# Token blocks of 2, 2, 3, 3, 3, 3 tiles instead of eight of 2 in a fused S4 + SwiGLU layer

## The chip, the core and the metric

One core of a Trainium2 chip runs the whole program. The metric is the device time of one execution, in microseconds (us). The engines are TensorE (PE, matmuls; PEld is its weight load), VectorE (DVE), ScalarE (ACT), GpSimd (POOL) and SyncE (SP), which here issues every DMA. Each engine works through its own instructions in the order in which they were written; PE runs weight loads ahead of its matmuls.

## The reference

A layer with two residual branches over 2048 tokens of width 448; the scales and shifts (sa, ca, ga, sb, cb, gb) come from one conditioning row.

```python
mod = (_silu(c) @ w_mod).reshape(c.shape[0], 6, 1, -1)
h = _layernorm(x) * (1 + ca) + sa
x = x + ga * S4(h, ...)                       # y = causal conv of h with K, plus h * Dskip
h = _layernorm(x) * (1 + cb) + sb
x = x + gb * ((_silu(h @ w_gate) * (h @ w_up)) @ w_down)      # F = 1792
```

K[d, l] is the real part of a sum over 256 complex exponentials. For inputs whose exponents are small enough (a flag computed on the chip) the kernel uses the first two moments of K, so that the convolution becomes running sums over the tokens. That path, small_path, is the one that runs here.

## The kernel before

Tokens come in 16 tiles of 128. A prelude computes the modulation rows, the moments and the branch of tiles 0 and 1 and starts the weight loads. Then run_blocks takes the tiles in blocks of two (BLOCKS, L23). For each block, ffn runs over 14 slices f of 128 hidden columns. gate_up(f) makes the gate and the up product, transposed, in PSUM banks of their own: for each of the two, 11 matmuls whose moving operand is 128 x (128 per tile) values of hhi or hlo, the high and low parts of the normalised tokens (L659). Then come SiLU on ACT (L665, output p), the product on VectorE (L670), its high part on ACT (L673, phi) and its low part on VectorE (L674, plo). down(f-1) follows gate_up(f) on PE and adds phi and plo times the high and low parts of w_down to one bank dn per tile (L685, three matmuls of 448 columns for each tile). So the chain L665 to L674 of one f has the time of the next gate_up.

In block 0 (fresh) the weights of f+2 are also split into parts (split_w, L97 to L102, and split_d, L90 and L91), and pools.load sends the loads of f+5 and, for w_down, of f+3 through SyncE's queue, into three rotating stages each. The parts stay in SBUF for all later blocks. After block 0 the stages raw (4 KB a partition each) and rawd are no longer used.

The branch of the next block's tiles is woven in by hand. TIMES (L29) has one row for the first block and one for all others. A number h in it means f = h // 2, before down(f-1) if h is even and behind it if odd. The steps of one tile in small_path are:
- n1.stat and n1.root: mean and variance on VectorE (L128, L129), the root on GpSimd.
- s0: h, two operations on VectorE. s1: v0 and v1, the products with two gain rows (L774; on GpSimd, in block 0 on VectorE).
- s2: the running sums are added to row 0 of v0 (L779, VectorE) and of v1 (L780, GpSimd). Then v0 is split into vh (ACT) and vl (VectorE).
- s3: h times gd (L789, GpSimd, in block 0 VectorE).
- s4: three matmuls with the triangular matrix into the PSUM tile cv and a bank (L795 to L797), and an addition on VectorE.
- s14 takes the place of s2 to s4 in block 0 (L803 to L813): v0 and v1 unsplit, and two matmuls more that add the running sums on PE (L809, L810). A float32 matmul counts as two in the profile.
- s5: the new running sums (ACT L819, VectorE L820), sent to row 0 by a small DMA through SyncE's queue (L821), and two VectorE operations that finish the tile (L822, L823).
- n2.stat, n2.root and make_xn (ACT, L179): the second norm.

At f = 13, between gate_up(13) and down(12), transposes brings the next block's tiles into hhi and hlo: four groups, each into a PSUM tile, read by ACT (L187, L189) and VectorE (L191, L192). All four PSUM tiles come from bank(), four banks in rotation, which gate_up and s4 use too; each gate_up takes two. The other four banks are dn0, dn1, dn2 and cv. dn2 serves the first gate product and two small matmuls. In the prelude, cv is the output of the six L436 matmuls that come right behind the first transposes and make the first running sums.

At the end of a block VectorE scales and adds (L711, L712) and SyncE sends the tile out (L713). xbuf holds four token tiles; load_x (L63) loads the next block's tiles at the block's start.

Of the kernel before, what the change touches and what calls it, by code (L numbers as in the profile page):

```python
# [19 lines left out]
NF = F // 128  # L20
NP0 = 3
NS = 3
BLOCKS = [2] * 8  # L23
TILES = [list(range(sum(BLOCKS[:b]), sum(BLOCKS[:b + 1]))) for b in range(len(BLOCKS))]
MB = max(BLOCKS)

TIMES = (  # L29
    (3, (4, 6, 9, 10, 12), (7, 8, 16, 17, 18), 19, (20, 21)),  # L30
    (3, (4, 5, 9, 11, 12, 13, 14), (6, 8, 16, 17, 18, 19, 20), 21, (22, 23)),
)
EPS = 1e-5

# [4 lines left out]
def f32(ap):  # L39
    return ap.bitcast(F32)  # L40
# [3 lines left out]
def tile_kernel(ctx, tc, x, a_re, a_im, b_re, b_im, c_re, c_im, log_dt, dskip,  # L44
# [10 lines left out]
    def bank():  # L55
        t = psg.tile([128, 512], F32, name="bank")
        return t

    xs = {}
    xbuf = [const.tile([128, D], F32, name=f"x{q}") for q in range(2 * MB)]  # L60
    gb = const.tile([128, D], F32)

    def load_x(i):  # L63
# [6 lines left out]
    wgu, raw, wdn, wp = {}, {}, {}, {}  # L70
    stage = [const.tile([128, 2, 4, 128], F32, name=f"raw{q}") for q in range(NS)]
    stage_d = [const.tile([128, D], F32, name=f"rawd{q}") for q in range(NS)]

    def load_w(pool, j):
        wgu[j] = pool.tile([128, 2, 7, 128], F32R, name=f"gu{j}")
# [92 lines left out]

    xn = {}

    def make_xn(i, new, src=None, on_v=False):
        src = xs[i] if src is None else src
        xn[i] = new()
        m, rs, ng = n2.of[i]
        for o, a, n in ((0, 0, D), (D, 384, 64)):
            if on_v:
                ve.tensor_scalar(xn[i][:, o:o + n], src[:, a:a + n], m, rs, op0=OP.subtract, op1=OP.mult)
            else:
                sc.activation(xn[i][:, o:o + n], src[:, a:a + n], AF.Identity, scale=rs, bias=ng)  # L179

    def transposes(ts):
        n = len(ts) * 128
        for k in range(4):
            ps = bank()
            for j, i in enumerate(ts):
                pe.transpose(ps[:, j * 128:(j + 1) * 128], xn[i][:, k * 128:(k + 1) * 128], ident)  # L186
            sc.activation(hhi[:, k, 0:n], ps[:, 0:n], AF.Identity, scale=cb1c[:, k:k + 1], bias=sbc[:, k:k + 1])  # L187
            if k % 2:
                sc.activation(ps[:, 0:n], ps[:, 0:n], AF.Identity, scale=cb1c[:, k:k + 1], bias=sbc[:, k:k + 1])  # L189
            else:  # L190
                ve.tensor_scalar(ps[:, 0:n], ps[:, 0:n], cb1c[:, k:k + 1], sbc[:, k:k + 1], op0=OP.mult, op1=OP.add)  # L191
            ve.tensor_tensor(hlo[:, k, 0:n], ps[:, 0:n], f32(hhi[:, k, 0:n]), op=OP.subtract)  # L192
# [61 lines left out]
    with tc.tile_pool(name="pre", bufs=1) as pre, tc.tile_pool(name="wm", bufs=6) as wm:  # L254
# [164 lines left out]
        n2.root(TILES[0])  # L419
        mod_col(sbc, sb_, 0.0)  # L420
        for q in range(2):
            make_xn(q, lambda: pre.tile([128, 512], F32, name="xn", bufs=2), os[q], q == 0)
            if q == 0:
                sc.copy(xs[q], os[q])
                mod_col(cb1c, row, 1.0)
# [22 lines left out]
    def general_conv():  # L448
# [3 lines left out]
        with tc.tile_pool(name="gh", bufs=2) as gh:  # L452
            t = gh.tile([P, 4, D], F32, name="wga")
            sy.dma_start(t, w_group(2))
            sc.copy(g0, mod_row([t[:, k, :] for k in range(4)]))
            for i in range(NT):
                load_x(i)
                n1.all([i])
                h = gh.tile([128, D], F32, name="h")
                make_h(h, i)  # L460
                sy.dma_start(hd[i * 128:(i + 1) * 128, :], h)
# [172 lines left out]

    def run_blocks(pools, stages, first=None):
        work, hid = pools.work, pools.hid
        new_xn = lambda: work.tile([128, 512], F32, name="xn", bufs=MB)
        def ffn(ts, fresh, last, todo):
            n = len(ts) * 128
            dn = [psd.tile([128, 512], F32, name=f"dn{q}") for q in range(len(ts))]  # L640
# [3 lines left out]
            def gate_up(f, nw):  # L644
                head = fresh and f == 0
                if fresh and not head:
                    split_d(f)
                w = wgu[f]
                p = hid.tile([128, MB * 128], F32, name="p")
                hi = hid.tile([128, MB * 128], F32R, name="phi")  # L650
                lo = hid.tile([128, MB * 128], F32R, name="plo")
                ps = [psd.tile([128, 512], F32, name="dn2") if head else bank(), bank()]

                def mm(s, lo):

                    parts = ((0,), (1,), (2,), (6,)) if lo else ((0, 3), (1, 4), (2, 5), (6,))
                    for k, ws in enumerate(parts):
                        for a in ws:
                            pe.matmul(ps[s][:, 0:n], w[:, s, a], (hlo if lo else hhi)[:, k, 0:n],  # L659
                                      start=not lo and a == 0, stop=lo and k == 3)  # L660

                for s, z in ((0, False), (1, False), (0, True), (1, True)) if head else (
                        (0, False), (0, True), (1, False), (1, True)):
                    mm(s, z)
                sc.activation(p[:, 0:n], ps[0][:, 0:n], AF.Silu)  # L665
                if head:
                    split_d(f)
                elif nw is not None:
                    split_w(nw, 0)
                ve.tensor_tensor(ps[1][:, 0:n], p[:, 0:n], ps[1][:, 0:n], op=OP.mult)  # L670
                if nw is not None and not head:
                    split_w(nw, 1)
                sc.copy(hi[:, 0:n], ps[1][:, 0:n])  # L673
                ve.tensor_tensor(lo[:, 0:n], ps[1][:, 0:n], f32(hi[:, 0:n]), op=OP.subtract)  # L674
                if nw is not None:
                    split_w(nw, None if head else 2)
                pp[f] = hi, lo
# [25 lines left out]
            else:  # L703
                down(NF - 1, qz)
            for q, i in enumerate(ts):
                t = new_xn()[:, 0:D]

                h = D // 2 if last and q == len(ts) - 1 else D
                for a in range(0, D, h):
                    c_ = slice(a, a + h)  # L710
                    ve.tensor_tensor(t[:, c_], dn[q][:, c_], gb[:, c_], op=OP.mult)  # L711
                    ve.tensor_tensor(xs[i][:, c_], xs[i][:, c_], t[:, c_], op=OP.add)  # L712
                    sy.dma_start(out[i * 128:(i + 1) * 128, c_], xs[i][:, c_])  # L713
# [3 lines left out]
        if first is not None:  # L717
            for i in TILES[1]:
                load_x(i)
            for i in TILES[0]:  # L720
                first(i)
                n2.stat(i, TILES[0])
            n2.root(TILES[0])
            for i in TILES[0]:
                make_xn(i, new_xn)
            transposes(TILES[0])
        for b, ts in enumerate(TILES):
            todo = {}
            if b + 1 < len(TILES):
                nx = TILES[b + 1]  # L730

                def at(f, late, g, *a):
                    todo.setdefault((f, late), []).append((g, a))

                if b:
                    for i in nx:
                        at(0, 1, load_x, i)
                root1, *times, root2, shift = TIMES[min(b, 1)]
                st = stages(b == 0)

                def go(h, g, *a):
                    at(h // 2, h % 2, g, *a)

                for q, (i, hs) in enumerate(zip(nx, times)):
                    at(1 if b else q, 1, n1.stat, i, nx)
                    for h, g in zip(hs, st):
                        go(h, g, i)
                    go(hs[-1], n2.stat, i, nx)
                go(root1, n1.root, nx)
                go(root2, n2.root, nx)  # L750
                for h, i in zip(shift, nx):
                    go(h, make_xn, i, new_xn)
                at(NF - 1, 0, transposes, nx)
                if b == 0:
                    at(2, 1, end_gate)
            ffn(ts, b == 0, b + 1 == len(TILES), todo)

    def small_path(pools):
# [15 lines left out]
                (ve if on_v else po).tensor_tensor(v, h, g, op=OP.mult)  # L774
            vs[i] = h, v0, v1

        def s2(i):
            h, v0, v1 = vs[i]
            ve.tensor_tensor(v0[0:1], v0[0:1], run0[0:1], op=OP.add)  # L779
            po.tensor_tensor(v1[0:1], f32(v1[0:1]), run1[0:1], op=OP.add)  # L780
            vh = work.tile([128, D], F32R, name="vh")
            vl = work.tile([128, D], F32R, name="vl")
            sc.copy(vh, v0)
# [15 lines left out]
            vs[i] = o, s  # L799

        def s14(i):  # L803
            h, v0, v1 = vs[i]
            o = psd.tile([128, 512], F32, name="cv")[:, 0:D]
            s = bank()[:, 0:D]
            pe.matmul(o, f32(tri), v0, start=True, stop=False)
            pe.matmul(s, tri, v1, start=True, stop=False)
            pe.matmul(s, f32(tri[0:1, :]), run1[0:1], start=False, stop=True)  # L809
            pe.matmul(o, f32(tri[0:1, :]), run0[0:1], start=False, stop=True)  # L810
            s3(i, True)
            ve.tensor_tensor(xs[i], h, xs[i], op=OP.add)
            vs[i] = o, s  # L813
# [8 lines left out]
            ve.tensor_tensor(xs[i], xs[i], o, op=OP.add)  # L822
            ve.scalar_tensor_tensor(xs[i], s, tok, xs[i], op0=OP.mult, op1=OP.add)  # L823

        return lambda fresh: (s0, lambda i: s1(i, True), s14, s5) if fresh else (s0, s1, s2, s3, s4, s5)

    def general_path(pools, y):
        work = pools.work
# [17 lines left out]
            s0(i)  # L846
            s1(i)

        return lambda fresh: (s0, s1), first

    class Pools:
        def __init__(self, es):
# [56 lines left out]
```

## Time and profile before

| | |
|---|---|
| runs of the kernel (us) | 518.09, 519.38, 519.93; median 519.38 |
| the profiled execution | 519.4, its span 517.6 |
| prelude up to f=0 | 0 to 49.8 |
| block 0 | 49.8 to 113.9 |
| blocks 1 to 6 | 57.1 each |
| block 7, PE's part, and the rest | 456.5 to 510.2, and to 517.6 |
| mean granted PE clock | 0.982 |

The profile lists, for one execution, each engine's busy time, groups of instructions by source line with their shapes, waits with what ended them, and the chain of work that ended last, followed back from the end. In the chain, rows are start, length, and what ran; matmuls of one line in a row are merged, so that length divided by count is the spacing. A timeline row is start, length, engine, line, operation, output<-inputs, count and, in brackets, idle time before it with its releaser. A wait row is who waited <- for whom: total us, times, longest. A group row ends with busy us, mean ns of one, and idle us before it. Matmuls overlap, so the mean duration of one is longer than the spacing.

### The profile page before, as it was taken

The numbers are of one execution on the slowest core, as the hardware profiler recorded it, in microseconds if no ns is written. First come the engines' busy times: TensorE is split into PE (matmuls) and PEld (weight loads), VectorE is DVE, ScalarE is ACT, GpSimd is POOL, SyncE is SP. The second block draws the span as 40 slices with busy tenths as digits, with TensorE's granted clock in tenths as the row PEclk, the third lists the DMA queues.
The fourth block names the chain that finished last, engine by engine and source line by source line (L and its number), as shares of the span: only waits on it lengthen the run. The fifth ranks groups of instructions, "written<-read, shape, count | busy, mean of one in ns | idle before, by whom it ended". The sixth has DMA issues, their size and how long they took to land.

```text
span 517.6 us, 8533 instructions
## 1 busy us (share of the span) xinstructions
PE 493.8 (95%) x3371; PEld 461.8 (89%) x3371; DVE 286.1 (55%) x568; ACT 174.3 (34%) x414; POOL 102.0 (20%) x127
## 2 busy tenths in 40 slices
PE   7869999999999999999999999999999999999994
PEld 5446987999999999999998999989998999999993
DVE  2797797785553665455653655465555555252123
ACT  4347555552223322331225223331225222332110
POOL 1577000102311051103300051105210231100000
PEclk9977999999999999999999999999999999999998
DMA  7995455501000200010000200020000200010001
GB/s 209 277 220 160 138 157 153 166 15 58 2 2 0 73 1 0 2 48 26 0 2 1 71 1 2 2 71 2 2 2 0 72 1 0 3 37 1 0 2 42
DMA packets 26009, 26.15 MB, mean 51 GB/s; under 512 B 2248, under 2 KB 25288, under 8 KB 25960
## 3 DMA queue, kind: packets, MB, share of 16 engines
q1 hardware_dynamic: 25960, 25.52, 17.3%
q8 instruction: 28, 0.46, 0.4%
q14 instruction: 21, 0.17, 0.1%
HBM read 21.80 MB, written 3.67 MB: 49 GB/s over the span
## 4 chain that ended last, share of the span: by engine, by line
PE 90%; DVE 4%; DMA 2%; ACT 2%; issue 1%; SPq 0%; DVEq 0%
PE bank L659 56%; PE dn L685 26%; PE bank L203 2%; DMA dsk<-in_A_Dskip_dram 1%; PE dn L406 1%; PE bank L186 1%; DVE scr L350 1%; PE bank L236 1%; DMA run<-run 1%; DVE bank L670 1%; DVE plo L674 1%; DVE h L164 1%; ACT phi L673 1%; PE bank L796 0%; PE cv L797 0%
## 5 line engine op out<-in xcount | busy, mean ns | idle before, releaser
L659 PE MATMUL bank<-hhi,gu 128*128 128x256 f32 x1561 | 223.9, 283 | 0.0
L659 PEld LDWEIGHTS bank<-hhi,gu 128*128 128x128 f32 x1561 | 210.1, 191 | 4.2 <-ACT phi L673 0.7
L659 PE MATMUL bank<-hlo,gu 128*128 128x256 f32 x892 | 143.4, 283 | 0.0
L670 DVE TENSOR_TENSOR bank<-p,bank 128x256 f32<-128x256 f32 x112 | 47.9, 428 | 142.8 <-PE bank L659 141.7
L659 PEld LDWEIGHTS bank<-hlo,gu 128*128 128x128 f32 x892 | 123.1, 192 | 0.0
L673 ACT CAST phi<-bank 128x256 fp32r<-128x256 f32 x112 | 41.7, 372 | 144.8 <-DVE bank L670 144.8
L665 ACT ACTIVATE p<-bank 128x256 f32<-128x256 f32 x111 | 42.4, 382 | 129.2 <-PE bank L659 128.9
L674 DVE TENSOR_TENSOR plo<-bank,phi 128x256 fp32r<-128x256 f32 x112 | 47.4, 423 | 44.3 <-ACT phi L673 44.3
L685 PE MATMUL dn<-wdh,phi 128*128 128x448 f32 x224 | 64.9, 370 | 0.0
L685 PE MATMUL dn<-wdl,phi 128*128 128x448 f32 x224 | 63.9, 366 | 0.0
L685 PE MATMUL dn<-wdh,plo 128*128 128x448 f32 x224 | 63.8, 365 | 0.0
L685 PEld LDWEIGHTS dn<-wdh,plo 128*128 128x128 f32 x224 | 42.0, 188 | 3.5
L685 PEld LDWEIGHTS dn<-wdl,phi 128*128 128x128 f32 x224 | 42.0, 188 | 3.3
L685 PEld LDWEIGHTS dn<-wdh,phi 128*128 128x128 f32 x224 | 36.1, 191 | 1.7 <-ACT gu L98 0.7
L145 POOL TENSOR_SCALAR rsa<-mva 128x2 f32<-128x2 f32 x8 | 2.0, 251 | 143.3 <-DVE mva L129 143.3
L780 POOL TENSOR_TENSOR v<-v,run 1x448 fp32r<-1x448 f32 x12 | 13.8, 1146 | 49.6 <-DMA run<-run 49.6
L145 POOL TENSOR_SCALAR rsb<-mvb 128x2 f32<-128x2 f32 x8 | 1.8, 220 | 108.1 <-DVE mvb L129 108.1
L774 POOL TENSOR_TENSOR v<-h,gm 128x448 f32<-128x448 f32 x12 | 13.8, 1153 | 25.3 <-DVE h L166 25.3
L186 PE MATMUL bank<-ident,xn 128*128 128x128 f32 x64 | 10.9, 296 | 6.2 <-DVE plo L674 5.5
L203 PE MATMUL bank<-wmt,cs 112*128 112x448 f32 (+1 forms) x32 | 15.1, 624 | 1.6 <-DMA wmt<-in_w_mod_dram 1.6
L187 ACT ACTIVATE hhi<-bank,sbc,cb1c 128x256 fp32r<-128x256 f32 x32 | 16.5, 575 | 0.3 <-PE bank L186 0.3
L789 POOL TENSOR_TENSOR h<-h,gd 128x448 f32<-128x448 f32 x12 | 16.4, 1365 | 0.0
(178 smaller groups left out, 437.3 us busy)
## 6 DMA issues: line engine op xcount, KB each, us to landing
wmt<-in_w_mod_dram SPq DMA_DIRECT2D x6, 784.0 KB
x<-in_A_u_dram SPq DMA_DIRECT2D x16, 224.0 KB
out_dram<-x SPq DMA_DIRECT2D x15, 224.0 KB
rawd<-in_B_w_down_dram SPq DMA_DIRECT2D x14, 224.0 KB
raw<-in_B_w_gate_dram SPq DMA_DIRECT2D x14, 192.0 KB
raw<-in_B_w_up_dram SPq DMA_DIRECT2D x14, 192.0 KB
raw<-in_B_w_gate_dram SPq DMA_DIRECT2D x14, 64.0 KB
raw<-in_B_w_up_dram SPq DMA_DIRECT2D x14, 64.0 KB
```

The lines of the kernel that those rows point to most:

```text
L186: pe.transpose(ps[:, j * 128:(j + 1) * 128], xn[i][:, k * 128:(k + 1) * 128], ident)
L187: sc.activation(hhi[:, k, 0:n], ps[:, 0:n], AF.Identity, scale=cb1c[:, k:k + 1], bias=sbc[:, k:k + 1])
L203: pe.matmul(ps[0:rows, 0:D], cs[:, k:k + 1].to_broadcast([P, rows]), w[k], start=k == 0, stop=k == 3)
L659: pe.matmul(ps[s][:, 0:n], w[:, s, a], (hlo if lo else hhi)[:, k, 0:n], start=not lo and a == 0, stop=lo and k == 3)
L665: sc.activation(p[:, 0:n], ps[0][:, 0:n], AF.Silu)
L670: ve.tensor_tensor(ps[1][:, 0:n], p[:, 0:n], ps[1][:, 0:n], op=OP.mult)
L673: sc.copy(hi[:, 0:n], ps[1][:, 0:n])
L674: ve.tensor_tensor(lo[:, 0:n], ps[1][:, 0:n], f32(hi[:, 0:n]), op=OP.subtract)
L685: pe.matmul(dn[q][:, 0:D], u[:, cs], v, start=f == 0 and z == 0, stop=f == NF - 1 and z == 2)
L774: (ve if on_v else po).tensor_tensor(v, h, g, op=OP.mult)
L780: po.tensor_tensor(v1[0:1], f32(v1[0:1]), run1[0:1], op=OP.add)
L789: (ve if on_v else po).tensor_tensor(h, h, gd, op=OP.mult)
```

## The change

Blocks become 2, 2, 3, 3, 3, 3 tiles, so there are six instead of eight, and the gate and up matmuls of the last four have 384 moving columns. A third down bank, dn2, is used there. TIMES has a row for block 0, one for block 1 (two tiles wide, with three tiles' branches woven in) and one for the rest.

Room in SBUF: xbuf has six tiles, two of them the spent rawd stages; make_xn writes to halves of spent raw stages (xn_of), and p of blocks 1 to 5 lies in another (p_of). The third of the four transpose groups goes to cv instead of a rotating bank, in the prelude too.

The branch: in block 0, s14 gives way to rows (the additions of the running sums, both on VectorE) and s4f, which has no running sums to add on PE. In block 1 s1, s2 and s3 run on VectorE alone. Later blocks use the steps as they were.

```diff
-BLOCKS = [2] * 8
+BLOCKS = [2, 2, 3, 3, 3, 3]
...
-    (3, (4, 6, 9, 10, 12), (7, 8, 16, 17, 18), 19, (20, 21)),
-    (3, (4, 5, 9, 11, 12, 13, 14), (6, 8, 16, 17, 18, 19, 20), 21, (22, 23)),
+    ((1, 3), 3, ((4, 6, 7, 9, 10, 12), (8, 11, 14, 16, 17, 18)), 19, (20, 21)),
+    ((3, 4, 5), 5, ((6, 7, 8, 10, 10, 12, 14), (9, 11, 15, 17, 17, 18, 19), (13, 16, 20, 19, 21, 22, 22)), 23, (24, 24, 25)),
+    ((3, 3, 3), 4, ((6, 7, 9, 10, 11, 12, 13), (8, 9, 14, 15, 16, 17, 18), (12, 13, 19, 19, 21, 22, 22)), 23, (24, 24, 25)),
...
-    xbuf = [const.tile([128, D], F32, name=f"x{q}") for q in range(2 * MB)]
+    xbuf = [const.tile([128, D], F32, name=f"x{q}") for q in range(4)]
...
+    xbuf += stage_d[0:2 * MB - 4]
+    spare = [t.rearrange("p a b c -> p (a b c)") for t in stage]
+    xn_of = [spare[2][:, 0:512], spare[2][:, 512:1024], spare[0][:, 0:512]]
+    p_of = [spare[1][:, q * 512:q * 512 + MB * 128] for q in range(2)]
...
-            ps = bank()
+            ps = psd.tile([128, 512], F32, name="cv") if k == 2 else bank()
...
-                p = hid.tile([128, MB * 128], F32, name="p")
+                p = hid.tile([128, 256], F32, name="p") if fresh else p_of[f % 2]
...
-        def s2(i):
+        def rows(i, on_v=False):
             h, v0, v1 = vs[i]
             ve.tensor_tensor(v0[0:1], v0[0:1], run0[0:1], op=OP.add)
-            po.tensor_tensor(v1[0:1], f32(v1[0:1]), run1[0:1], op=OP.add)
+            (ve if on_v else po).tensor_tensor(v1[0:1], f32(v1[0:1]), run1[0:1], op=OP.add)
+
+        def s2(i, on_v=False):
+            rows(i, on_v)
...
-        def s14(i):
+        def s4f(i):
             h, v0, v1 = vs[i]
             o = psd.tile([128, 512], F32, name="cv")[:, 0:D]
             s = bank()[:, 0:D]
-            pe.matmul(o, f32(tri), v0, start=True, stop=False)
-            pe.matmul(s, tri, v1, start=True, stop=False)
-            pe.matmul(s, f32(tri[0:1, :]), run1[0:1], start=False, stop=True)
-            pe.matmul(o, f32(tri[0:1, :]), run0[0:1], start=False, stop=True)
+            pe.matmul(s, tri, v1, start=True, stop=True)
+            pe.matmul(o, f32(tri), v0, start=True, stop=True)
...
+        v = lambda g: lambda i: g(i, True)
+        return lambda b: ((s0, v(s1), v(rows), s4f, s5), (s0, v(s1), v(s2), v(s3), s4, s5),
+                          (s0, s1, s2, s3, s4, s5))[min(b, 2)]
```

In a row of the new TIMES stand the half steps of n1.stat, of n1.root, then for each tile those of its steps with n2.stat last, then n2.root and make_xn.

More of the change, by code (lines that the diff above doesn't have):

```diff
@@ L169, in tile_kernel, with make_xn @@
     xn = {}
-    def make_xn(i, new, src=None, on_v=False):
+    def make_xn(i, to, src=None, on_v=False):
         src = xs[i] if src is None else src
-        xn[i] = new()
+        xn[i] = to
         m, rs, ng = n2.of[i]
@@ L421, in tile_kernel @@
         for q in range(2):
-            make_xn(q, lambda: pre.tile([128, 512], F32, name="xn", bufs=2), os[q], q == 0)
+            make_xn(q, pre.tile([128, 512], F32, name="xn", bufs=2), os[q], q == 0)
             if q == 0:
@@ L456, in general_conv @@
             for i in range(NT):
-                load_x(i)
+                xs[i] = xbuf[i % 4]
+                sy.dma_start(xs[i], x[i * 128:(i + 1) * 128, :])
                 n1.all([i])
@@ L636, in run_blocks @@
         work, hid = pools.work, pools.hid
-        new_xn = lambda: work.tile([128, 512], F32, name="xn", bufs=MB)
         def ffn(ts, fresh, last, todo):
@@ L705, in ffn @@
             for q, i in enumerate(ts):
-                t = new_xn()[:, 0:D]
+                t = xn_of[q][:, 0:D]
                 h = D // 2 if last and q == len(ts) - 1 else D
@@ L723, in run_blocks @@
             n2.root(TILES[0])
-            for i in TILES[0]:
-                make_xn(i, new_xn)
+            for q, i in enumerate(TILES[0]):
+                make_xn(i, work.tile([128, 512], F32, name=("h", "v0")[q], bufs=2))
             transposes(TILES[0])
@@ L737, in run_blocks @@
                         at(0, 1, load_x, i)
-                root1, *times, root2, shift = TIMES[min(b, 1)]
-                st = stages(b == 0)
+                stat1, root1, times, root2, shift = TIMES[min(b, 2)]
+                st = stages(b)
                 def go(h, g, *a):
                     at(h // 2, h % 2, g, *a)
[L744 to L748, printed above, removed]
-                go(root1, n1.root, nx)
+                for i, h in zip(nx, stat1):
+                    go(h, n1.stat, i, nx)
+                go(root1, n1.root, nx)
+                for h, q, z in sorted((h, q, z) for q, hs in enumerate(times) for z, h in enumerate(hs)):
+                    if z < len(times[q]) - 1:
+                        if z < len(st):
+                            go(h, st[z], nx[q])
+                    else:
+                        go(h, n2.stat, nx[q], nx)
                 go(root2, n2.root, nx)
-                for h, i in zip(shift, nx):
-                    go(h, make_xn, i, new_xn)
+                for q, (h, i) in enumerate(zip(shift, nx)):
+                    go(h, make_xn, i, xn_of[q])
                 at(NF - 1, 0, transposes, nx)
@@ L775, in s1 @@
             vs[i] = h, v0, v1
-        def s2(i):
+        def rows(i, on_v=False):
             h, v0, v1 = vs[i]
             ve.tensor_tensor(v0[0:1], v0[0:1], run0[0:1], op=OP.add)
-            po.tensor_tensor(v1[0:1], f32(v1[0:1]), run1[0:1], op=OP.add)
+            (ve if on_v else po).tensor_tensor(v1[0:1], f32(v1[0:1]), run1[0:1], op=OP.add)
+        def s2(i, on_v=False):
+            rows(i, on_v)
+            h, v0, v1 = vs[i]
             vh = work.tile([128, D], F32R, name="vh")
@@ L823, in s5 @@
             ve.scalar_tensor_tensor(xs[i], s, tok, xs[i], op0=OP.mult, op1=OP.add)
-        return lambda fresh: (s0, lambda i: s1(i, True), s14, s5) if fresh else (s0, s1, s2, s3, s4, s5)
+        v = lambda g: lambda i: g(i, True)
+        return lambda b: ((s0, v(s1), v(rows), s4f, s5), (s0, v(s1), v(s2), v(s3), s4, s5),
+                          (s0, s1, s2, s3, s4, s5))[min(b, 2)]
     def general_path(pools, y):
@@ L847, in first @@
             s1(i)
-        return lambda fresh: (s0, s1), first
+        return lambda b: (s0, s1), first
     class Pools:
```

## The prediction

> **What bounds the kernel now.** I read the page's busy time and chain first, then the chain in order of time over one block, then the same stretch by windows.
>
> ```profile
> span 517.6 us, 8533 instructions
> ```
> ```profile
> PE 493.8 (95%) x3371; PEld 461.8 (89%) x3371; DVE 286.1 (55%) x568; ACT 174.3 (34%) x414; POOL 102.0 (20%) x127
> ```
> ```profile
> PE bank L659 56%; PE dn L685 26%; PE bank L203 2%; DMA dsk<-in_A_Dskip_dram 1%; PE dn L406 1%; PE bank L186 1%; DVE scr L350 1%; PE bank L236 1%; DMA run<-run 1%; DVE bank L670 1%; DVE plo L674 1%; DVE h L164 1%; ACT phi L673 1%; PE bank L796 0%; PE cv L797 0%
> ```
> ```profile
> 168.60 2.44 PE dn L685 x12
> 171.04 5.27 PE bank L659 x44
> 176.31 1.22 PE dn L685 x6
> 177.53 2.64 PE bank L659 x22
> ```
> ```profile
> 45.00:50.00 5.00, 4.34 (x16) 3.11 (x16) 3.80 (x8) 4.72 (x12) 4.57 (x4) 0.51 0.64 203
> 50.00:54.00 4.00, 4.00 (x29) 4.00 (x28) 1.34 (x3) 2.36 (x6) 0.00 (x0) 0.76 0.43 124
> ...
> 113.94:171.04 57.10, 56.31 (x409) 54.68 (x408) 30.84 (x63) 17.25 (x42) 11.73 (x14) 1.00 0.06 17
> ```
>
> Two matmul lines carry 82% of the chain. The chain rows give their spacing: 5.27 us / 44 = 119.8 ns for a gate/up matmul of 256 columns, 2.44 / 12 = 203.3 ns for a down matmul of 448. (Window columns: us; busy time of PE, PEld, DVE, ACT, POOL; granted clock; DMA share; GB/s.) A block of two tiles lasts 57.10 us with PE busy for 56.31 at clock 1.00, VectorE for 30.84. It adds up: 14 x 22 x 119.8 ns = 36.9, 14 x 6 x 203.3 = 17.1, six branch matmuls 1.2, together 55.2; the remaining 1.9 are eight transposes and one wait. So a part of the change is worth what it does to PE's stream; other engines count where PE waits for them.
>
> **The change part by part.**
>
> *Wider blocks.* Twelve tiles move from six blocks of two to four of three. Down, branch and transpose matmuls stay the same in number; gate/up goes from 6 x 308 = 1848 matmuls of 256 columns to 4 x 308 = 1232 of 384. No row shows 384. A line through 119.8 at 256 and 203.3 at 448 gives 175.5 ns: 1848 x 119.8 = 221.4 us become 1232 x 175.5 = 216.2, **-5.2**. Bounds: cost by column as at 256 (179.7 ns) saves nothing; as at 448 (174.3 ns) saves 6.6. I take the line, as 384 lies between two measured widths.
> The Trainium skill (TensorE: Matmul & The Clock Gate, Back-to-back issue gap) puts only 2.5 ns of a warm gap outside the columns; 616 matmuls fewer would then save an estimated 1.5 us, but its 109 and 189 ns for these widths are below the measured 119.8 and 203.3.
>
> *The bank for the transposes.*
>
> ```profile
> 166.56 0.82 PE L186 MATMUL bank<-ident,xn 128*128 128x128 f32 x6
> 166.82 0.43 DVE L670 TENSOR_TENSOR bank<-p,bank 128x256 f32<-128x256 f32 x1 [2.55 <-PE bank L659]
> ...
> 167.68 0.42 DVE L674 TENSOR_TENSOR plo<-bank,phi 128x256 fp32r<-128x256 f32 x1 [0.44 <-ACT phi L673]
> ...
> 168.16 0.44 PE L186 MATMUL bank<-ident,xn 128*128 128x128 f32 x2 [0.79 <-DVE plo L674]
> ```
> ```profile
> PE bank L186 <- DVE plo L674: 5.5, 7, 0.8
> ```
>
> The fourth group of transposes takes the bank that L674 of the last f still reads, and PE idles 0.79 us at each of seven boundaries. With the third group in cv, the fourth takes the bank that SiLU read, free before PE comes. What is late next is the evacuation of the transposes, under 12 down matmuls (2.44 us) now and 18 (3.7 us) behind three tiles, while its ACT and DVE pieces grow with 384/256; the reserve stays. **-5.5** for seven waits (five removed, two boundaries gone); if half of it returned as a wait for the evacuation, -2.8.
>
> *The same line in the prelude.* cv is also the output of the L436 matmuls, which follow the first tiles' transposes at once and now have to wait for cv's last reader.
>
> ```profile
> 45.82 1.75 PE bank L186 x7
> 47.57 2.24 PE cv L436 x6
> 49.81 1.49 PE dn L659 x7
> ```
> ```profile
> 48.88 0.75 DVE L192 TENSOR_TENSOR hlo<-bank,hhi 128x256 fp32r<-128x256 f32 x2
> ```
> ```profile
> SPq L79 <- DVE gu L100: 3.5, 2, 2.4
> ```
>
> That reader is the first of the two L192 at 48.88, done near 49.3. L436 starts there and not at 47.3 (its first matmul overlaps the transposes' modelled end), so gate/up of f=0 starts about 2.0 us later. In the next loads SyncE waits for L100's split of f=0 (2.4 us), so the weight stream moves by as much, and block 0 has no reserve to swallow it (below): **+2.0**. Bounds: 0, and +3.1, if the clock, at 0.51 and 0.76 in the two windows, comes up so late that all 22 matmuls of f=0 run at 1.49 / 7 = 213 ns, where now 14 do.
> The Trainium skill (the same page, What's actually happening) has the clock released after about 3.4 us of sustained activity; a gap of 2 us in it speaks for the upper end, and the time would be an estimated 1.1 us above mine.
>
> *Block 0's branch.* s14 becomes two row additions on VectorE and three passes on PE instead of seven.
>
> ```profile
> 69.63 0.75 PE cv L807 x2
> ...
> 72.28 2.83 PE bank L659 x22
> ```
> ```profile
> 84.50 3.85 DMA run<-run
> 88.35 0.04 issue
> 88.39 1.01 PE bank L809 x2
> 89.41 0.75 PE cv L810 x2
> 90.16 1.41 PE dn L685 x6
> ```
>
> For its first tile PE spends 2.65 us (69.63 to 72.28); the new one needs about 0.95 (two passes as the L810 pair, 0.75, and one of 0.2), but waits some 1.3 for the additions, queued behind the products that end only as PE arrives. The 0.5 us won is lost again at the second tile: its running sum is issued at 84.50 behind SyncE's weight loads and lands at 88.35, while PE stands. Now PE resumes 1.8 us after landing; then the row additions (0.60 each, L779 below, 1.25 together) come first, then 0.95 of PE: 2.2. **+0.4**; bounds -0.6 (the first tile's gain survives) and +1.5 (L670 and the weight splits, queued on VectorE behind the waiting additions, hold PE as well).
>
> *Block 1: two tiles wide, three tiles' branches, on VectorE.*
>
> ```profile
> 147.80 0.42 DVE L674 TENSOR_TENSOR plo<-bank,phi 128x256 fp32r<-128x256 f32 x1 [0.44 <-ACT phi L673]
> 148.14 0.60 DVE L779 TENSOR_TENSOR v<-v,run 1x448 f32<-1x448 f32 x1
> ...
> 148.83 0.57 ACT L783 CAST vh<-v 128x448 fp32r<-128x448 f32 x1 [1.06 <-DVE v L779]
> ...
> 149.43 0.62 DVE L784 TENSOR_TENSOR vl<-v,vh 128x448 fp32r<-128x448 f32 x1 [0.69 <-ACT vh L783]
> ```
> ```profile
> 152.64 0.63 DVE L820 SCALAR_TENSOR_TENSOR run<-run,cv 32x448 f32<-32x448 f32 x1
> 153.29 0.62 DVE L822 TENSOR_TENSOR x<-x,cv 128x448 f32<-128x448 f32 x1
> ```
> ```profile
> 156.48 0.62 DVE L128 BATCH_NORM_STATS2 stb<-x 128x6 f32<-128x448 f32 x1
> 157.13 0.18 DVE L129 BATCH_NORM_AGGREGATE mvb<-stb 128x2 f32<-128x6 f32 x1
> ```
>
> The three extra branch matmuls and four transposes are moved in from later blocks: no sum. For the third tile s2 stands at half step 20 (f=10, before the down matmuls) and s4 at 21 (behind them): one group of 1.22 us between, where the old table had two half steps or more. L674 starts 1.1 us after gate/up ends (166.56 to 167.68) and vl ends 2.25 us after L674's start (147.80 to 150.05): vl at 3.4. VectorE is also behind: f=9 gives it s5 (3 x 0.65, by the spacing of 152.64 and 153.29), s3 (0.65) and a stat (0.8), 3.4 us on top of 1.5 up to the step behind L674, against PE's period of 3.86, so with what f=8 leaves L670 of f=10 starts about 1.1 late. PE gets through s4 at 3.4 + 1.1 + 0.2 = 4.7 instead of 1.22 + 0.61 = 1.8, with gate/up of f=11 queued behind it: **+2.9**. Bounds: 0, and 4.0, if VectorE is late by one us more. The other two tiles have two half steps or more, and vl comes just in time.
>
> *The end.*
>
> ```profile
> 510.16 0.63 DVE xn L711
> ...
> 510.82 0.62 DVE x L712
> ```
>
> The last block has a third tile to scale, add and send: 1.3 us more on VectorE, which starts on the first tile 0.6 us earlier against PE's end: **+0.6** (0.4 to 1.0).
>
> *At nothing.*
>
> ```profile
> L789 POOL TENSOR_TENSOR h<-h,gd 128x448 f32<-128x448 f32 x12 | 16.4, 1365 | 0.0
> L774 POOL TENSOR_TENSOR v<-h,g 128x448 fp32r<-128x448 f32 x12 | 13.9, 1160 | 0.0
> ```
>
> Tokens in spent weight stages are loaded at the block's start and read in f=1, as now, and a wide f is 1.8 us longer; late ones would hold VectorE at the first stat, and PE one f later. p in a spent stage changes only its place. GpSimd's branch in blocks 2 to 5 has at most four operations between two steps that need them, 4.8 us, and these lie two half steps, 22 x 175.5 ns + 9 x 203.3 = 5.7 us, apart; without that reserve VectorE would wait in s4 and PE, as above, some 2 us a block.
>
> **The sum:** -5.2 - 5.5 + 2.0 + 0.4 + 2.9 + 0.6 = -4.8 us on a span of 517.6: 512.8. The profiled execution took 519.4, 1.8 more than its span, and the median of the runs is 519.38; the forecast is **514.6 us**.
>
> **Rivals.** *Nothing waits in front or in block 1.* If the prelude's gap vanishes behind block 0's wait for the running sum, and VectorE runs ahead in block 1: 514.6 - 2.0 - 2.9 = 509.7. For it: PE stands still at 84.5 to 88.4 anyway. Against: that wait ends with the load stream, which moves too, and s2 and s4 are half a step apart.
> *The matmul costs by column.* Then 384 saves nothing: 514.6 + 5.2 = 519.8. For it: 203.3 / 448 and 119.8 / 256 are within 3% of each other. Against: that 3% is the whole gain and is measured at clock 1.00. The skill's back-to-back rule would come near this, at an estimated 518.3.
> *VectorE bounds block 1.* If, from f=4 to f=8, its work in one f stays above PE's 3.86 us, vl of the first two tiles also comes one f late, and PE waits 3.5 us for each: 514.6 + 7.0 = 521.6, slower. By the rows f=6 and f=7 have 4.4 to 4.6 us of work, f=5 and f=8 less than PE's time with s4 in it: late by one us, made good again. It decides once an operation costs 0.75 us rather than 0.65, or a running sum, which holds the whole queue, lands late.
>
> **How the numbers follow.** The forecast has 0.58 (its own range 512 to 518), nothing waits 0.18, cost by column 0.12, VectorE bounds 0.12. A measurement of this kernel tells about 0.3%, 1.6 us, from no change. Faster: 0.18 and 0.56 of the first; slower: 0.11; within: the rest, 0.15. The range goes from 508.5 (below the second case, for a width gain of 6.6) to 520.5 (past the third); the last is left out.
>
> **What would show it.** L659 on 384 columns near 175 ns; no wait of L186 for L674; L436 starting near 49.3 and f=0 near 51.7; a run<-run piece still in block 0's chain; in block 1 a wait of L796 or L797 for vl at f=10, some 3 us, and none at the others; wide blocks of about 83 us with PE never idle. The forecast fails if 384 columns cost under 174 or over 179 ns, if wide blocks show waits of their own, or if VectorE's queue stops PE at more than one place of block 1.

## The result and the profile after

The changed kernel takes 517.4 us (median of 20 runs), the kernel before 519.9 in the same rounds: a ratio of 0.9936, 95% interval 0.9914 to 0.9958. The profiled span goes from 517.6 to 514.7 us. The forecast was 514.6 us, a gain of 4.8. The direction held, and a part of the gain came: 2.5 us by the medians, 2.9 by the spans, 3.3 by the ratio. The time lies inside the range of 512 to 518, 0.6 us from its upper end.

The page of the changed kernel first: the span, the granted clock in 40 slices, and the lines of the chain.

```profile
span 514.7 us, 7042 instructions
```
```profile
PEclk8888999899998999999999999999999999999998
```
```profile
PE bank L665 51%; PE dn L691 24%; SPq L85 3%; SPq L86 2%; DMA br<-in_A_B_re_dram 2%; DMA raw<-in_B_w_up_dram 1%; PE bank L192 1%; DMA run<-run 1%; DVE gu L106 1%; DVE gu L108 1%; SPq L275 1%; DMA rawd<-in_B_w_down_dram 1%; DVE wdl L97 1%; DVE bank L676 1%; PE cv L809 1%
```

Two slices near 90 and 160 us show 8 for the clock, where the page before had 9 from block 0 to the last slice but one:

```profile
PEclk9977999999999999999999999999999999999998
```

(Line numbers have moved: L665 is the old L659, L691 the old L685, L192 the old L186.) The chain of a wide block, in order of time:

```profile
437.17 3.82 PE bank L665 x22
440.99 1.85 PE dn L691 x9
...
499.58 3.82 PE bank L665 x22
```

Eleven f take 499.58 - 437.17 = 62.41 us, 5.67 each; the forecast had 5.69. Of the two-wide 3.85 us, one and a half are 5.78. Now what PE waits for in the changed kernel (its list of waits, PE's rows):

```profile
...
PE bank L820 <- DVE v L790: 3.9, 2, 3.0
PE cv L442 <- DVE hlo L198: 2.9, 1, 2.9
...
PE cv L809 <- ACT vh L797: 2.2, 1, 2.2
...
PE bank L192 <- ACT raw L185: 1.0, 2, 0.7
```

The waits of the transposes for plo are gone. In their place stand block 0's additions of the running sum (L820 is s4f), the prelude's cv (L442), block 1's vh (L809) and, at block 1's end, the new tokens (L185 is make_xn). The timeline around L809:

```profile
161.55 0.47 PE L809 MATMUL cv<-vh,tri 128*128 128x448 f32 x1 [2.21 <-ACT vh L797]
161.86 0.37 PE L810 MATMUL bank<-v,tri 128*128 128x448 f32 x1
162.21 0.47 PE L811 MATMUL cv<-vl,tri 128*128 128x448 f32 x1
162.52 1.33 PE L665 MATMUL bank<-hhi,gu 128*128 128x256 f32 x7
163.65 1.05 PE L665 MATMUL bank<-hlo,gu 128*128 128x256 f32 x4
164.50 1.70 PE L665 MATMUL bank<-hhi,gu 128*128 128x256 f32 x7
```

Seven matmuls that take 1.00 us elsewhere take 1.70 here, behind the wait. The windows tell why (us; busy time of PE, PEld, DVE, ACT, POOL; granted clock; DMA share; GB/s): the two long waits, each with the stretch behind it.

```profile
88.70:91.70 3.00, 0.04 (x1) 0.00 (x0) 1.66 (x5) 1.40 (x3) 0.00 (x0) 0.93 0.52 155
91.70:95.40 3.70, 3.68 (x9) 2.68 (x10) 3.60 (x7) 1.62 (x5) 0.00 (x0) 0.59 0.65 191
159.30:161.50 2.20, 0.04 (x1) 0.00 (x0) 1.70 (x4) 0.94 (x2) 0.00 (x0) 1.00 0.00 0
161.50:166.60 5.10, 5.05 (x25) 4.67 (x26) 1.16 (x2) 0.39 (x1) 0.00 (x0) 0.67 0.01 3
```

The clock granted to PE falls to 0.59 and 0.67 on average behind a wait of 3.0 and one of 2.2 us. So a wait can have a second price, paid after it ends, that the forecast weighed for the prelude alone.

### The profile page after: what moved, and what is told of

Its sections match the earlier page's. It is cut to its first block, busy times and chain, and to the rows that moved or that the text cites. A ratio compares the mean times of both kernels' runs of the same rounds, so it can differ in the third digit from the quotient of the medians.

```text
span 514.7 us, 7042 instructions
## 1 busy us (share of the span) xinstructions
PE 485.2 (94%) x2747; PEld 453.5 (88%) x2747; DVE 278.3 (54%) x516; ACT 163.9 (32%) x346; POOL 87.3 (17%) x103
## 4 chain that ended last, share of the span: by engine, by line
PE 79%; DVE 6%; SPq 6%; DMA 4%; issue 3%; ACT 1%; POOL 0%; DVEq 0%; ACTq 0%; POOLq 0%
PE bank L665 51%; PE dn L691 24%; SPq L85 3%; SPq L86 2%; DMA br<-in_A_B_re_dram 2%; DMA raw<-in_B_w_up_dram 1%; PE bank L192 1%; DMA run<-run 1%; DVE gu L106 1%; DVE gu L108 1%; SPq L275 1%; DMA rawd<-in_B_w_down_dram 1%; DVE wdl L97 1%; DVE bank L676 1%; PE cv L809 1%
## 5 line engine op out<-in xcount | busy, mean ns | idle before, releaser
L665 PE MATMUL bank<-hhi,gu 128*128 128x384 f32 (+1 forms) x1169 | 211.3, 320 | 0.0
L665 PEld LDWEIGHTS bank<-hhi,gu 128*128 128x128 f32 x1169 | 191.6, 190 | 3.4 <-issue 0.7
L665 PE MATMUL bank<-hlo,gu 128*128 128x384 f32 (+1 forms) x668 | 131.9, 318 | 0.0
L676 DVE TENSOR_TENSOR bank<-raw,bank 128x384 f32<-128x384 f32 (+1 forms) x70 | 37.5, 535 | 154.3 <-PE bank L665 137.7
L665 PEld LDWEIGHTS bank<-hlo,gu 128*128 128x128 f32 x668 | 110.3, 190 | 0.3 <-DVE hlo L198 0.3
L679 ACT CAST phi<-bank 128x384 fp32r<-128x384 f32 (+1 forms) x84 | 37.3, 444 | 145.1 <-DVE bank L676 145.1
L671 ACT ACTIVATE raw<-bank 128x384 f32<-128x384 f32 (+1 forms) x70 | 32.8, 469 | 128.7 <-PE bank L665 128.5
L680 DVE TENSOR_TENSOR plo<-bank,phi 128x384 fp32r<-128x384 f32 (+1 forms) x84 | 43.0, 512 | 38.0 <-ACT phi L679 38.0
L691 PE MATMUL dn<-wdh,phi 128*128 128x448 f32 x224 | 61.3, 373 | 0.5 <-ACT phi L679 0.5
L691 PE MATMUL dn<-wdl,phi 128*128 128x448 f32 x224 | 60.0, 368 | 0.0
L691 PE MATMUL dn<-wdh,plo 128*128 128x448 f32 x224 | 59.9, 367 | 0.0
L691 PEld LDWEIGHTS dn<-wdl,phi 128*128 128x128 f32 x224 | 42.3, 189 | 4.0
L691 PEld LDWEIGHTS dn<-wdh,plo 128*128 128x128 f32 x224 | 41.9, 188 | 4.1
L691 PEld LDWEIGHTS dn<-wdh,phi 128*128 128x128 f32 x224 | 39.9, 190 | 2.6 <-ACT phi L679 1.1
L106 DVE TENSOR_TENSOR gu<-raw,gu 128x768 fp32r<-128x768 f32 x14 | 14.6, 1041 | 0.4 <-ACT gu L103 0.3
L797 ACT CAST vh<-v 128x448 fp32r<-128x448 f32 x12 | 6.8, 567 | 20.7 <-DVE v L789 20.7
```

Of the source, the lines that this page charges most:

```text
L106: ve.tensor_tensor(lo, w[:, :, 0:3, :], f32(hi), op=OP.subtract)
L691: pe.matmul(dn[q][:, 0:D], u[:, cs], v, start=f == 0 and z == 0, stop=f == NF - 1 and z == 2)
```

## The experiments

All times are medians beside runs of the kernel before on the same chip; the ratio is to that kernel, and the range behind it is its 95% interval. Times out of traces are those of one profiled execution for each run, which need not be the median one. As the prelude of one profiled execution starts f=0 up to 2.7 us earlier or later than that of another (46.90 to 49.61 us in nine executions with the same prelude), lengths of blocks are compared, from the first gate/up row of one block to that of the next.

### The prelude's bank

```diff
-            ps = psd.tile([128, 512], F32, name="cv") if k == 2 else bank()
+            ps = psd.tile([128, 512], F32, name="cv") if k == 2 and spare_bank else bank()
...
-        transposes(TILES[0])
+        transposes(TILES[0], False)
```

> The changed kernel, but the prelude's third transpose group takes a rotating bank again. Carried theory: f=0 starts 2.0 us earlier (49.7), SyncE's loads and the landing of run<-run in block 0 move with it (to about 88.4), and the whole kernel gains 2.0 us: some 515.4 us beside 517.4. Rival, hidden: block 0 waits for the running sum anyway, which lands at the same 90.5, and the time stays within 0.5 us.

514.2 us, ratio 0.9878 (0.9843 to 0.9914). The changed kernel's L442 waited 2.90 us, without anything to do for PE:

```profile
49.43 0.93 PE L442 MATMUL cv<-vh,left 128*33 128x448 f32 x2 [2.90 <-DVE hlo L198]
```

Without the wait f=0 starts at 48.87 and not at 51.65, the running sum of block 0 is issued at 84.14 and not at 86.62, and block 1 starts at 114.76 and not at 116.92. The loss was carried, as the first theory had it, 2.2 us out of 2.8: the weight loads hang on f=0, and the running sum behind them. PE still waits in block 0 (3.75 us now and not 2.98, as it comes earlier).

### Block 1: s2 half a step earlier

```diff
-(13, 16, 20, 19, 21, 22, 22)
+(13, 16, 19, 19, 21, 22, 22)
```

> The changed kernel with one number of TIMES changed: s2 of block 1's third tile one half step earlier (20 to 19), behind the down matmuls of f=9. Theory of the half step: PE's wait for vh before L809 falls from 2.2 us to about 1.0, and if it gets short enough for the clock to stay up, gate/up of f=11 goes back from 4.14 to 2.63 us: 1.2 to 2.7 us gained. Rival, VectorE has no time left in block 1: the wait moves to another place and the time stays within 0.5 us.

514.26 us, ratio 0.9882 (0.9846 to 0.9918). Block 1 goes from 62.82 (116.92 to 179.74) to 59.66 us (117.70 to 177.36), and the clock stays up:

```profile
160.66 0.47 PE L809 MATMUL cv<-vh,tri 128*128 128x448 f32 x1 [0.53 <-ACT vh L797]
160.96 0.37 PE L810 MATMUL bank<-v,tri 128*128 128x448 f32 x1
161.31 0.47 PE L811 MATMUL cv<-vl,tri 128*128 128x448 f32 x1
161.62 1.00 PE L665 MATMUL bank<-hhi,gu 128*128 128x256 f32 x7
```

It was the half step, and not VectorE's load: one number of the table was worth 3.2 us, more than the 2.7 expected at most.

### PE kept busy in its waits

```diff
+                if b < 2:
+                    go((16, 21)[b], warm, (11, 8)[b])
                 for h, q, z in sorted(...)
```

> The changed kernel with matmuls that nobody reads in PE's two long waits: 11 of 512 columns ahead of s4f of block 0's second tile, 8 ahead of s4 of block 1's third. Clock theory: the matmuls behind these waits are slow because the granted clock falls to 0.5 when PE stands still; with PE busy it stays at 1.00, gate/up of f=11 in block 1 takes 2.63 us and not 4.14, the passes and down matmuls behind s4f run at full speed, and 2 to 3 us are gained. Rival, the matmuls are slow because their operands come late: nothing gained, or up to 0.5 us lost to the fillers.

513.87 us, ratio 0.9859 (0.9821 to 0.9897). The windows of this run over the same two places:

```profile
92.00:95.40 3.40, 3.40 (x19) 2.92 (x20) 3.30 (x7) 1.27 (x5) 0.00 (x0) 1.00 0.70 202
158.00:160.30 2.30, 1.98 (x9) 1.31 (x7) 1.81 (x4) 0.93 (x2) 0.00 (x0) 1.00 0.00 0
160.30:165.00 4.70, 4.64 (x31) 4.19 (x32) 1.59 (x3) 0.70 (x3) 0.00 (x0) 1.00 0.00 0
```

The clock stays at 1.00, though the operands come no earlier. In block 0, from s4f's first pass to the next gate/up takes 2.26 us (91.96 to 94.22) instead of 3.69 (91.72 to 95.41); block 1 takes 61.32 instead of 62.82. Some 2.9 us of the changed kernel's profiled execution were the clock alone; by the ratios the fillers gained 4.0.

### Block 0's branch as before

```diff
-((1, 3), 3, ((4, 6, 7, 9, 10, 12), (8, 11, 14, 16, 17, 18)), 19, (20, 21)),
+((1, 3), 3, ((4, 6, 9, 10, 12), (7, 8, 16, 17, 18)), 19, (20, 21)),
...
-((s0, v(s1), v(rows), s4f, s5), ...
+((s0, v(s1), s14, s5), ...
```

> The changed kernel with block 0's branch as before: s14 at its old half steps, the running sums added on PE. By the prediction's own step (0.4 us for the additions that come first): 0.4 us gained. Theory of the clock: s14 issues its three passes over v0 and v1 ahead of the wait, so that PE stands still for less than 1 us instead of 3.0, the clock stays up, and 1.5 to 2 us are gained. Rival, the weight loads set block 0's end either way: nothing.

515.18 us, ratio 0.9895 (0.9859 to 0.9932), an interval that overlaps that of the changed kernel. The profiled execution is the fastest of its six. From the landing of the running sum to the next gate/up takes 3.0 us (90.49 to 93.52) instead of 4.9 (90.52 to 95.41). s14 has its three passes over v0 and v1 behind it when the wait begins, so PE stands still for 1.5 us and not 3.0:

```profile
88.29 0.71 PE L831 MATMUL bank<-v,tri 128*128 128x448 f32 x1
90.49 1.01 PE L832 MATMUL bank<-run,tri 1*128 1x448 f32 x2 [1.49 <-DMA run<-run]
```

The version with fewer passes put all of them behind the wait. What that costs without the clock is seen where the clock stays up behind s4f: with the fillers it takes 3.55 us from landing to the next gate/up (90.67 to 94.22), so some 0.5 of the 1.9 us are the order of the work and 1.4 the clock. Nor does the old order keep the clock up by itself. The same wait of 1.5 us, with the same passes ahead of it, stands in five more traces below, and in four of them the clock falls behind it (the table in the last section).

This run showed something else. Block 1 has the same wait of 2.21 us at L809 as the changed kernel, but here the clock stays up behind it:

```profile
157.40:159.60 2.20, 0.06 (x1) 0.00 (x0) 1.71 (x4) 0.93 (x2) 0.00 (x0) 1.00 0.00 0
159.60:164.00 4.40, 4.34 (x29) 3.92 (x30) 1.59 (x3) 0.40 (x3) 0.00 (x0) 1.00 0.00 0
```

Block 1 took 61.32 us, as with the fillers. The same wait cost 1.5 us more in the changed kernel, in the run with the prelude's bank and in the one without the spare bank below.

### All three together

Two versions have the prelude's bank and s14; they differ in block 1's row. The first moves two tiles and the norm half a step forward, so that no step has to hurry:

```diff
-((3, 4, 5), 5, ((6, 7, 8, 10, 10, 12, 14), (9, 11, 15, 17, 17, 18, 19), (13, 16, 20, 19, 21, 22, 22)), 23, (24, 24, 25)),
+((3, 3, 4), 4, ((5, 6, 7, 9, 9, 11, 13), (8, 10, 14, 16, 16, 17, 18), (12, 15, 19, 19, 21, 22, 22)), 23, (24, 24, 25)),
```

> The changed kernel with three edits: the prelude's transposes on rotating banks, block 0's branch as before (s14), and block 1's row of TIMES moved: the first two tiles one half step earlier, the third tile's s2 at 19 with s4 still at 21, so that two half steps lie between. If the three losses stand beside each other they add: 2.0 (prelude), 1.9 (block 0), 3.2 (block 1), and the wait of the transposes for the new tokens at block 1's end, 1.0, goes too as the third tile's chain no longer starts late: 7 to 8 us under the changed kernel, about 509.5 beside 517.4. Rival, they overlap, because the weight loads set the end of block 0 or VectorE that of block 1: 4 us or less.

510.86 us, ratio 0.9828 (0.9802 to 0.9855). PE has no wait left in block 1 but the last:

```profile
PE bank L832 <- DMA run<-run: 1.5, 1, 1.5
PE bank L192 <- ACT raw L185: 1.0, 2, 0.7
```

The gain against the changed kernel's 0.9936 is 5.6 us, under the 7 to 8 expected. Block 1 fell to 58.59 us, but the wait for the new tokens stayed, against my expectation; it does not come from the chain's lateness. And the prelude and block 0 gave less than the 3.9 us expected of them: block 1 starts at 115.35 and not at 116.92. Behind the wait of 1.5 us in block 0 the clock fell to 0.50, two us after PE had gone on, and one f of gate/up took 3.98 us and not 2.63:

```profile
91.11 1.55 PE dn L691 x6
92.66 3.98 PE bank L665 x22
```

So the losses did not simply add, and the rival's 4 us or less did not come either.

> As e5_shifted, but block 1's row of TIMES changed in one number alone (the third tile's s2 from 20 to 19). If the losses add: 2.0 + 1.9 + 3.2 = 7.1 us under the changed kernel, some 0.5 to 1 us behind e5_shifted, as PE's wait of 0.5 us for vh and the 1.0 us for the new tokens stay. Rival as there: 4 us or less.

511.63 us, ratio 0.9827 (0.9802 to 0.9853). With only the one number changed, PE waits 1.4 us at L809 here, and 0.53 in the run that changed this number alone: in this execution the second tile's running sum took longer to land, and s2, one half step behind it, held VectorE's queue:

```profile
156.10 2.92 DMA run<-run
```

The tight place costs now more, now less; the shifted table does not have it. By the medians the two cannot be told apart. This version is the sum of three runs above. The prelude's bank and the one number gained 0.58% and 0.54% beside the changed kernel, which would give a ratio of 0.9824 without s14; with it, 0.9827 was measured. The intervals are too wide to say that s14 brings nothing, but it isn't shown that its 0.4% comes on top.

### The bank alone, and everything but the bank

The kernel before, with the one line at the boundaries:

> The kernel before with the third transpose group in cv at the block boundaries alone (the prelude as it was). By the prediction's term: seven waits of 0.79 us go, 5.5 us under the kernel before, ratio 0.989. Rival, the evacuation of the transposes is late next and takes half of it back: 2.8 us or less.

513.21 us, ratio 0.9886 (0.9860 to 0.9912): better than the whole change.

```profile
168.83 5.27 PE bank L659 x44
222.48 2.44 PE dn L685 x12
224.91 5.27 PE bank L659 x44
```

A block takes 56.08 us instead of 57.10: 1.02 us a boundary, where the prediction took 0.79 from PE's wait. Weight loads waited 1.03 us at the same place before; PE's idle time is counted from a modelled end, and a stream that breaks off is not in it. The row of the kernel before:

```profile
PEld bank L186 <- DVE plo L674: 7.2, 7, 1.0
```

Seven boundaries make 7.1 us by the block lengths; the run's time moved by 4.6 to 7.3.

> The changed kernel with all four transpose groups on rotating banks, in the prelude and at the boundaries. Against e1_prelude_bank, which differs in the boundaries alone: five waits of L192 for plo come back, 0.8 us each after two tiles and about the same after three, where the chain to plo is longer but three transposes a group pass first: 4 us slower than e1_prelude_bank, 2 us slower than the changed kernel. Rival, behind three tiles the wait is covered by the longer transposes: at most 1.6 us slower than e1_prelude_bank, from the two boundaries behind two tiles.

520.22 us, ratio 1.0003 (0.9980 to 1.0026): without the bank, the rest of the change brings nothing. Behind three tiles the wait is there too:

```profile
257.18 0.55 PE L192 MATMUL bank<-ident,raw 128*128 128x128 f32 x3 [0.85 <-DVE plo L680]
```

A wide block takes 83.61 us (261.38 to 344.99) instead of 82.54 (262.58 to 345.12): 1.07 us a boundary. Against the run that keeps the bank at the boundaries, 1.25% are 6.5 us; 4 had been expected, and five times 1.07 are 5.3. Block 0 of this run holds a wait of 3.65 us ahead of s4f, the second longest of all, and the clock stays at 1.00 behind it.

### The new tokens on two engines

```diff
-                    go(h, make_xn, i, xn_of[q])
+                    go(h, make_xn, i, xn_of[q], None, b == 1 and q > 0)
```

> As e5_shifted, but at block 1's end make_xn of the second and third tile runs on VectorE, which stands idle for 4.2 us there, and not on ScalarE behind the first. Theory: the transposes wait 1.0 us for three tiles' tokens made one after another, 1.04 us each, on one engine; split over two they are ready as PE comes, and the span from block 1's first f to block 2's falls from 58.6 to some 57.5 us: 1 us under e5_shifted. Rival: the wait passes to SiLU and the evacuation behind it, and nothing is gained.

507.78 us, ratio 0.9773 (0.9748 to 0.9799). Block 1 goes from 58.59 to 57.13 us (111.68 to 168.81), 1.5 us less. PE's row had shown 1.0, but the weight loads had stood for 0.62 and 0.84 us, as at the bank:

```profile
169.21 0.14 PEld L192 LDWEIGHTS bank<-ident,raw 128*128 128x128 f32 x1 [0.62 <-ACT raw L185]
170.19 0.42 PEld L192 LDWEIGHTS bank<-ident,raw 128*128 128x128 f32 x4 [0.84 <-ACT raw L185]
```

(These are rows of the run with the shifted table.) A plain block of two with the bank takes 56.08; three branch passes more are 0.62 and four transposes 0.44, together 57.14: nothing is lost in block 1 any more. By the ratios the gain is 2.9 us, but the two runs come from different chips; beside the next experiment, on the same chip and with the old make_xn, it is 1.7.

### GpSimd in block 1

```diff
-(s0, v(s1), v(s2), v(s3), s4, s5),
+(s0, s1, s2, s3, s4, s5),
```

> As e5_shifted, but block 1's s1, s2 and s3 use GpSimd as in the later blocks. If a block two tiles wide needs VectorE's 0.62 us an operation: GpSimd's 1.15 to 1.37 us make v1 or h late at s4 of at least one tile, and block 1 gets 2 to 4 us longer than e5_shifted's 58.6. Rival: GpSimd, idle there, keeps pace with half steps of 1.2 and 2.6 us and takes load off VectorE: 58.6 us or less.

509.52 us, ratio 0.9808 (0.9779 to 0.9836). Block 1 takes 58.80 us (114.20 to 173.00) instead of 58.59. With the shifted table, GpSimd keeps pace, and moving the branch to VectorE brought nothing that can be measured here. With the table of the change this was not tried.

### The running sum on a queue of its own

```diff
-            sy.dma_start(run[0:1], run[127:128])
+            (po if i in TILES[1] else sy).dma_start(run[0:1], run[127:128])
```

> As e9_xn_on_vector, but in block 0 the running sum is sent from GpSimd's queue and not behind the weight loads in SyncE's. If the queue is what makes it late (ready near 80, issued near 85.5, landed near 89.3 in e5_shifted): it lands before PE comes, PE's wait of 1.5 us at L832 goes, and block 0 ends 1.5 us earlier, unless the loads of w_down then hold PE some us later. Rival, the loads set the end of block 0: the wait goes and the end of block 0 stays.

505.85 us, ratio 0.9736 (0.9710 to 0.9762), the fastest version here, 2.6% under the kernel before. The sum leaves soon after it is ready at 78.0:

```profile
78.64 0.76 POOL L844 DMA_DIRECT2D run<-run  x1 [17.43 <-DVE run L843]
```

In the run with make_xn on two engines, on SyncE, it was ready at 76.7 and issued at 83.22. PE's wait of 1.5 us is gone, and half of it comes back as a wait of 0.8 us for phi: ScalarE had stood 2.2 and 1.8 us for w_down parts and comes late. Block 0, from f=0 on, goes from 64.8 us (46.90 to 111.68) to 64.0 (48.53 to 112.57). The medians differ by 1.9 us with intervals that overlap; the trace explains 0.7 of it, the rest stays open. One candidate: the trace with 64.8 is one in which the clock stayed up behind the wait of 1.5 us. In three others with the same code for block 0 it fell, and block 0 took 65.0, 66.1 and 68.4 us. Without the wait there is nothing for it to fall behind; that this is the rest is not shown.

## Why the prediction was right, and by how much it was off

Terms in us; "measured" is from block lengths and from the experiments, for this pair of profiled executions:

| step | forecast | measured | how |
|---|---|---|---|
| wider blocks | -5.2 | -6.0 | 56 f of 5.67 for 84 of 3.85 |
| bank at the boundaries | -5.5 | -7.1 | 7 x 1.02, bank alone |
| cv in the prelude | +2.0 | +2.0 | f=0 from 49.61 to 51.65; carried on, by the first experiment |
| block 0's branch | +0.4 | +2.0 | block 0 from 64.3 to 65.3, with 1.0 of bank in it |
| block 1 | +2.9 | +5.7 | 62.8, for 56.1 + 1.1 |
| end | +0.6 | +0.7 | last matmul's start to the span's end, 7.2 to 8.0 |
| sum | -4.8 | -2.7 | span: -2.9 |

That the time lies inside the range is in part luck. Two terms gained 2.4 us more than forecast, and three lost 4.5 us more; the errors cancel by half.

*Wider blocks.* The f period was right to 0.02 us, but with two errors in it. 22 matmuls of 384 columns take 3.82 us, 173.6 ns each, below the lower bound of 174.3 and below the 174 under which the forecast was to fail, though to the good; nine down matmuls take 1.85 us, 206 ns each and not 203. The line through a gate/up row and a down row mixed two kinds of matmul: through the gate/up rows alone, 119.8 and 173.6, it gives 200.5 at 448, less than a down matmul takes. The rival of cost by column is out.

*The bank.* Right in mechanism, under-sized by reading PE's idle time and not PEld's. The prediction's own remainder of 1.9 us for eight transposes and one wait held the number: eight transposes take 0.88 where nothing waits (112.05 to 112.93 in the run with the shifted table), which leaves 1.0. Nothing was late next behind the transposes of two or three tiles.

*The prelude's cv.* Right in place, and that block 0 would not absorb it was shown. The size agrees by the luck of the pair: the kernel before has the latest f=0 of the nine executions with that prelude (mean 48.4), while the four with the group in cv start it at 50.7 to 51.8 (mean 51.3). That is 2.8 us, and the first experiment gained 3.0 by its ratio, near the upper bound of 3.1. In all four the clock stood at 0.50 for three us or more behind the wait, as that bound had it.

*Block 0.* Here a step failed. The additions in front of PE's passes were priced at 0.4 us as a matter of order on VectorE, and where the clock stays up they cost some 0.5. But they also put all of PE's work behind the wait: PE stood for 3.0 us, and the clock fell, for 1.4 us that had been put at nothing. That standing for 3.0 and not for 1.5 us is what made it fall is not shown: behind 1.5 us it fell in four runs, and behind 3.65 it once stayed up.

*Block 1.* The half step was found, with its wait: PE's loss at s4 was forecast as 2.9 us. The row at L809 says 2.2, but gate/up of f=11 starts at 162.52 where 159.79 was due (the last two down matmuls start at 158.77; 0.40 for them and 0.62 for s4, as in f=8): 2.7 us, as VectorE was late by 0.9 (L676 at 159.09 for 158.23) and not by 1.1. What failed is that this was all: the clock behind it cost 1.5 us, and the new tokens made one after another at the end 1.5, a place where only two tiles' tokens had been in the row before. 2.7, 1.5 and 1.5 make the 5.7 of the table. VectorE did not bound the block; that rival is out, and the one in which nothing waits too.

The clock was weighed in the prediction for the prelude's gap alone. The Trainium skill (TensorE: Matmul & The Clock Gate, What's actually happening) describes windows of about 3.4 us that run on by themselves. That fits a wait of 2.21 us that costs 1.5 us in three runs and nothing in a fourth, as it would depend on where the wait lies in a window. But the clock also fell behind waits of 1.5 us, less than half of such a window; no run here shows the windows, and what decides stays open.

## What to carry to other kernels

Where PE bounds a kernel, price a wait twice: by its length, and by what the clock may take behind it, here nothing or 1.5 us, and once 3.1, for 1.5 to 3.8 us of standing. Put the work that does not depend on a late operand ahead of the wait, even if there is more of it (0.5 us here); better, take the wait away or fill it. Read what a wait costs from the weight loads' row or from the start of the next stretch, as PE's own idle time was too short three times. One trace tells whether the clock fell in that execution, not whether it falls: compare several. And try the parts of a change one by one: here one line on PSUM banks brought 1.1%, and the wide blocks around it paid only once three places where they were woven too tightly had been mended.

## What the runs showed of the hardware

Whether the granted clock falls behind a wait of PE did not go by the wait's length alone. These are all waits of 1.3 us or more from f=0 on to the end of block 1, one trace for each run, with the mean granted clock over the 5 us behind them:

| PE's wait (us) | where | run | clock behind it |
|---|---|---|---|
| 1.37 | block 1, s4 | three edits | 1.00 |
| 1.48, 1.56 | block 0, s4f of the first tile | prelude's bank, no spare bank | 1.00 |
| 1.49, 1.53 | block 0, s14 of the second tile | block 0's branch as before, new tokens on two engines | 1.00 |
| 1.50, 1.51, 1.52, 1.56 | the same | shifted table, bank alone, GpSimd in block 1, three edits | 0.79, 0.82, 0.66, 0.55 |
| 2.21 | block 1, s4 | block 0's branch as before | 1.00 |
| 2.21, 2.21, 2.21 | the same | changed kernel, prelude's bank, no spare bank | 0.66 |
| 2.98, 3.51, 3.75 | block 0, s4f of the second tile | changed kernel, s2 half a step earlier, prelude's bank | 0.70, 0.50, 0.66 |
| 3.65 | the same | no spare bank | 1.00 |

Where it fell, it stood at 0.50, and the fall came at once or up to 3 us after PE had gone on. Behind the waits of 1.5 us in block 0, from PE's first pass to the end of the next gate/up took 5.7 us where the clock stayed, 7.1 to 7.2 in three traces where it fell, and 8.8 in the fourth. No wait of 1.1 us or less had a fall behind it. The clock stayed at 1.00 too when matmuls that nobody read filled the wait, so operands were not the cause.
